# Attention by two head pairs a step, four late token blocks placed by products, and one written order behind the last scores

## The chip, the cores and the metric

The kernel runs on one core of one Trainium2 chip. The metric is the time of one execution on the device, in microseconds (us). The core has TensorE (PE, matrix products and transposes into PSUM), VectorE (DVE), ScalarE (ACT), GpSimd (POOL) and SyncE (SP, which issues most DMAs here). Each engine works through its own instructions in order. PEld is the weight load of TensorE.

## What is computed

Three layers follow one another. Attention is sparse (a query sees 8 global keys and the last 96), its output is the input of a mixture of 8 experts with the two best of each token, and a dense layer with a mish-like activation ends it.

```
scores = scale * q @ k.T + bias          # keep: 8 global keys, 96 local ones
a = softmax(scores);  x = a @ v          # 2 x 768 tokens, 8 heads of 64 -> x is 1536 x 512
noisy = x @ w_gate + log1p(exp(x @ w_noise)) * noise
top2 = two largest of noisy;  top2_w = softmax of them
out[tokens of e] += top2_w * (relu(x @ w1[e]) @ w2[e])       # 8 experts, 512 -> 1024 -> 512
h = out @ w_in;  g = h * tanh(softplus(h));  result = g @ w_out   # 512 -> 2048 -> 512
```

## The kernel before

The 1536 tokens are 12 blocks `t` of 128. Attention takes a block in four steps, one for each pair of heads `hp`; the main loop (lines 734 to 745) calls `st_scores(t, hp)` and then `pipe.run()`. `Steps` (the name `pipe`) is a list of calls by due step: `st_scores` puts `st_exp` into the same step and `st_turn` two steps on, `st_turn` puts `st_av` one step on, `st_av` puts `st_x` one step on. So four steps lie between the scores of a head pair and its last transpose.

- `st_scores` makes two score products into two PSUM banks (`sp`), and VectorE turns each into logits with its smallest value (line 491; here called a reduce). `st_exp` is two exponentials on ScalarE (line 503).
- `st_turn` is four transposes (`tp`, line 516) and a ScalarE copy (`at`, 517). `st_av` is four products with the values (`xp`, 530) and a VectorE copy (`xt`, 534). `st_x` transposes back (`xr`, 541); behind the last head pair of a block come `xs` (548, the finished block), its store, the gate products (564) and, a step later, `st_logits` (576).
- Routing (`st_logits`, `st_route`, `st_rank`) is some 16 to 20 small VectorE operations for a group of blocks (`GROUPS`). They wait in `Fill` and are let out one or three at a time (`PACE`) behind reduces and copies. `st_rank` gives each token of the block its place in the list of an expert, and `lay` (689) is the 0/1 matrix of places of expert 0.
- The rows of expert 0 are gathered for blocks 0 to 8 (`st_first_list`, four indirect DMAs of GpSimd) and turned by products with the identity (`st_first_in`, 654). Blocks 9 to 11 (`LATE` = 9) are added by products of `xs`, split into a high and a low part (`xsh` on ScalarE, `xsl` on GpSimd, 559), with `lay` (`st_first_add`, 664). The result goes to `xgT` (669, 670), with which the first expert product (`first_layer`, 767 to 769) starts.
- Behind the last scores (t = 11, hp = 3) nothing new comes into the pipeline. `pipe.drain` runs what is due, step after step, and lets out what is left in `Fill`.
- Weights are loaded as 128x1024 pieces and split into a high part (`whi`, ScalarE, 264) and a low part (`wlo`, 267). Three of these splits come in blocks 5 to 7, with the low part on GpSimd; the later ones have it on VectorE.

Of the kernel before, what the change touches and what calls it, by code (L numbers as in the profile page):

```python
# [9 lines left out]
F32 = mybir.dt.float32  # L10
# [25 lines left out]
GROUPS = ((0,1,2,3),(4,5,6,7,8),(9,10),(11,))  # L36
MOST = max(len(g) for g in GROUPS)
LATE = 9
# [3 lines left out]
FIRST = (2, 4)  # L42
ORDER = ((0, (0,)), (2, (0,)), (0, (1,)), (2, (1,)), (0, (2, 3)), (2, (2, 3)))
# [65 lines left out]
class Steps:  # L109


    def __init__(self):
        self.at, self.now = {}, 0

    def put(self, ahead, fn, *a, rank=9):
        self.at.setdefault(self.now + ahead, []).append((rank, fn, a))

# [15 lines left out]
class Fill:  # L133
# [3 lines left out]
    def __init__(self):  # L137
        self.ops, self.later, self.hold = deque(), deque(), False
# [7 lines left out]
    def some(self, n, more=0):  # L146

        if not self.ops:
# [15 lines left out]
def build(tc, ctx, I, out, n_global, n_local, dbg=None):  # L164
# [189 lines left out]
    with ExitStack() as st:  # L354
        at1 = st.enter_context(tc.tile_pool(name="at1", bufs=1))
        ld = st.enter_context(tc.tile_pool(name="ld", bufs=2))
        ps_s = st.enter_context(tc.tile_pool(name="ps_s", bufs=PSS if NKP == 512 else 1, space=PSUM))
# [102 lines left out]
        rtc = ps_x.tile([P, 512], F32, name="rtc") if PSS == 2 else rtb  # L460
# [5 lines left out]
        xsp, lay, lgs, es = {}, {}, {}, {}  # L466
# [4 lines left out]
        def st_scores(t, hp):  # L471
# [3 lines left out]
            z = wk.tile([P, 2, NKM], F32, name="z", bufs=4 if early else 3)  # L475
            sm = wk.tile([P, 2], F32, name="sm", bufs=4)
            if hp == 0:
                sums[t] = wk.tile([P, H], F32, name="sums", bufs=3)
            sps = {}

            def product(h):
                sps[h] = ps_s.tile([P, NKP], F32, name="sp")
                hh = slice(h * D, (h + 1) * D)
                for c, kc, n in runs[i]:
                    T.matmul(sps[h][:, c:c + n], raw[t][hh, hp, :], ks[hh, hp, kc:kc + n],  # L485
                             start=(c % 512 == 0), stop=(c + n == nk or (c + n) % 512 == 0))

            for h in range(2):
                for k in ((0, 1) if h == 0 else ()) if NKP == 512 else (h,):
                    product(k)  # L490
                V.tensor_tensor_reduce(out=z[:, h, :nk], in0=sps[h][:, :nk], in1=table(i, 2 * hp + h), scale=-SCALE,
                                       scalar=3e38, op0=OP.add, op1=OP.min, accum_out=sm[:, h:h + 1])
                fill.some(PACE[t >= LATE], MORE[t >= LATE])
            if early and t == NT - 1 and hp == HP - 1:
                lay["chunks"] = [(*CHUNKS[c], d) for d0, cs in ORDER for c in cs for d in (d0, d0 + 1)]
                pipe.put(2, st_first_in, FIRST[0])
            pipe.put(0, st_exp, t, hp, z, sm)
            pipe.put(2, st_turn, t, hp, z, rank=0)

        def st_exp(t, hp, z, sm):  # L500
            nk = NK[t % NB]
            for h in range(2):
                A.activation(z[:, h, :nk], z[:, h, :nk], AF.Exp, bias=sm[:, h:h + 1], scale=-1.0,
                             accum_out=sums[t][:, 2 * hp + h:2 * hp + h + 1])

        def st_turn(t, hp, z):
            nk = NK[t % NB]
            nch = (nk + P - 1) // P
            at = wk.tile([P, (NKM + P - 1) // P, 2, P], F32, name="at")
            for c0 in range(0, nch, 2):  # L510
                cs = range(c0, min(nch, c0 + 2))
                tp = ps_t.tile([P, 2, 2, P], F32, name="tp")
                for c in cs:
                    col = 0 if c == 0 else nk - P * (nch - c)
                    for h in range(2):
                        T.transpose(tp[:, c - c0, h, :], z[:, h, col:col + P], ident)  # L516
                A.activation(at[:, c0:c0 + len(cs)], tp[:, :len(cs)], AF.Copy)
            pipe.put(1, st_av, t, hp, at, rank=2)
            if early and t == NT - 1 and hp == HP - 1:
                pipe.put(1, st_first_in, FIRST[1])  # L520

        def st_av(t, hp, at):
# [3 lines left out]
            xp = xpb[:, hp]  # L526
            for c in range(nch):
                kk = nk - P * (nch - 1) if c == 0 else P
                for h in range(2):
                    T.matmul(xp[h * D:(h + 1) * D, :], vt[:kk, c, (2 * hp + h) * D:(2 * hp + h + 1) * D],  # L530
                             at[:kk, c, h, :], start=(c == 0), stop=(c == nch - 1))
            if hp == 0:
                xts[t] = wk.tile([P, HP, P], F32, name="xt", bufs=2)
            V.tensor_copy(xts[t][:, hp, :], xp)
            fill.some(PACE[t >= LATE], MORE[t >= LATE])
            pipe.put(1, st_x, t, hp, rank=1)

        def st_x(t, hp):
            if hp == 0:
                xps[t] = ps_r.tile([P, HP, P], F32, name="xr")  # L540
            T.transpose(xps[t][:, hp, :], xts[t][:, hp, :], ident)
            if hp == 1:
# [3 lines left out]
            if hp == HP - 1:  # L546
# [4 lines left out]
                pipe.put(2 if t + 1 < NT else 0, nc.sync.dma_start, xd[1 + t * P:1 + (t + 1) * P, :], xs.rearrange("p h d -> p (h d)"))  # L551
                pipe.put(0, st_gate, t)
                if early and t >= LATE:
# [755 lines left out]
```

## Time and profile before

| | |
|---|---|
| median of 3 runs | 764.21 us (762.32 to 766.95) |
| profiled execution | 765.73 us, of which the span 763.9 us |
| attention, from the first scores to the last | 7.35 to 102.8 us of the span |
| behind the last scores, to the end of the first expert product | 102.8 to 126.7 us |
| experts, then dense layer | the rest |
| busy in the span | PE 724.5, PEld 636.3, DVE 601.4, ACT 384.9, POOL 162.8 us |

How to read it: the span is from the first to the last instruction of the profiled execution, and 1.8 us lie around it. TensorE is busy 95% of the span, so what can be saved is where it waits, where its clock is low, or where it does work that can be left out.

### The profile page before, as it was taken

The numbers are of one execution on the slowest core, as the hardware profiler recorded it, in microseconds if no ns is written. First come the engines' busy times: TensorE is split into PE (matmuls) and PEld (weight loads), VectorE is DVE, ScalarE is ACT, GpSimd is POOL, SyncE is SP. The second block draws the span as 40 slices with busy tenths as digits, with TensorE's granted clock in tenths as the row PEclk, the third lists the DMA queues.
The fourth block names the chain that finished last, engine by engine and source line by source line (L and its number), as shares of the span: only waits on it lengthen the run. The fifth ranks groups of instructions, "written<-read, shape, count | busy, mean of one in ns | idle before, by whom it ended". The sixth has DMA issues, their size and how long they took to land.

```text
span 763.9 us, 11872 instructions
## 1 busy us (share of the span) xinstructions
PE 724.5 (95%) x4257; PEld 636.3 (83%) x4257; DVE 601.4 (79%) x1297; ACT 384.9 (50%) x814; POOL 162.8 (21%) x167
## 2 busy tenths in 40 slices
PE   8999989999999999999999999888899999999995
PEld 4665669899998989899999987766789898989894
DVE  7677767986768575757676597999999999999985
ACT  5787742344444444444444446444555555555453
POOL 2012030210101020101100031555333424432221
PEclk9999989999999999999999999999999999999999
DMA  6677421556655564646554552311020111101001
GB/s 173 201 190 183 141 76 44 169 194 195 189 168 190 166 193 152 210 155 214 165 183 139 179 196 79 105 55 28 1 69 29 29 42 27 32 26 42 1 0 46
DMA packets 42935, 89.28 MB, mean 117 GB/s; under 512 B 5987, under 2 KB 18403, under 8 KB 42868
## 3 DMA queue, kind: packets, MB, share of 16 engines
q1 hardware_dynamic: 35412, 69.37, 29.4%
q0 software_dynamic: 4096, 13.11, 5.8%
q10 hardware_dynamic: 3360, 5.97, 2.1%
q8 instruction: 35, 0.57, 0.3%
q14 instruction: 32, 0.26, 0.1%
HBM read 75.32 MB, written 13.11 MB: 116 GB/s over the span
## 4 chain that ended last, share of the span: by engine, by line
PE 64%; DVE 18%; ACT 6%; DMA 6%; issue 4%; POOL 1%; ACTq 1%; POOLq 0%; DVEq 0%
PE hp L767 8%; PE hp L768 8%; PE hp L769 8%; DMA raw<-in_w_moe 5%; PE ac L1133 4%; PE ac L1134 4%; PE ac L1138 4%; PE sp L485 4%; PE ac L767 4%; PE ac L769 4%; PE ac L768 4%; PE xp L530 3%; PE tp L516 3%; DVE wlo L267 3%; DVE yT L1090 2%
## 5 line engine op out<-in xcount | busy, mean ns | idle before, releaser
L1106 POOL TENSOR_TENSOR yT<-yT 128x384 f32<-128x384 f32 (+1 forms) x68 | 71.5, 1051 | 191.0 <-DVE yT L1105 173.3
L767 PE MATMUL hp<-xgh,whi 128*128 128x416 f32 (+1 forms) x288 | 104.3, 362 | 0.0
L267 DVE TENSOR_TENSOR wlo<-raw,whi 128x1024 fp32r<-128x1024 f32 x61 | 74.6, 1223 | 34.8 <-ACT whi L264 34.1
L769 PE MATMUL hp<-xgh,wlo 128*128 128x416 f32 (+1 forms) x288 | 100.8, 350 | 0.0
L768 PE MATMUL hp<-xgl,whi 128*128 128x416 f32 (+1 forms) x288 | 100.7, 350 | 0.0
L767 PE MATMUL ac<-hhi,whi 128*128 128x416 f32 x256 | 91.7, 358 | 0.0
L768 PE MATMUL ac<-hlo,whi 128*128 128x416 f32 x256 | 90.0, 352 | 1.5 <-DVE hlo L814 1.5
L769 PE MATMUL ac<-hhi,wlo 128*128 128x416 f32 x256 | 89.8, 351 | 0.0
L1109 ACT ACTIVATE hhi<-yT 128x384 fp32r<-128x384 f32 (+1 forms) x68 | 34.4, 506 | 93.8 <-POOL yT L1106 93.8
L314 POOL DMA_INDIRECT xg<-xd,gidx x32 | 32.2, 1005 | 219.7 <-PE tq L801 196.9
L767 PE MATMUL hp<-xgh,whil 128*128 128x384 f32 x224 | 76.4, 341 | 0.0
L768 PE MATMUL hp<-xgl,whil 128*128 128x384 f32 x224 | 75.7, 338 | 0.5 <-DVE xgl L773 0.5
L769 PE MATMUL hp<-xgh,wlol 128*128 128x384 f32 x224 | 75.3, 336 | 0.0
L264 ACT ACTIVATE whi<-raw 128x1024 fp32r<-128x1024 f32 x64 | 67.5, 1054 | 8.5 <-ACT ys L849 6.9
L1090 DVE SCALAR_TENSOR_TENSOR yT<-yT 128x384 f32<-128x384 f32 (+1 forms) x68 | 63.2, 929 | 2.3
L1133 PE MATMUL ac<-whil,hhi 128*128 128x512 f32 x144 | 58.2, 404 | 2.1 <-ACT hhi L1109 2.0
L813 ACT ACTIVATE hhi<-hp 128x416 fp32r<-128x416 f32 x64 | 32.6, 510 | 49.0 <-PE hp L769 46.7
L1134 PE MATMUL ac<-wlol,hhi 128*128 128x512 f32 x144 | 56.6, 393 | 0.0
L768 PEld LDWEIGHTS hp<-xgl,whi 128*128 128x128 f32 x288 | 54.3, 189 | 0.9 <-DVE xgl L670 0.3
L767 PEld LDWEIGHTS hp<-xgh,whi 128*128 128x128 f32 x288 | 54.1, 188 | 0.8
L769 PEld LDWEIGHTS hp<-xgh,wlo 128*128 128x128 f32 x288 | 54.0, 188 | 0.5
L295 ACT ACTIVATE whil<-t 128x512 fp32r<-128x512 f32 x26 | 16.4, 633 | 73.5 <-DVE t L301 65.9
(241 smaller groups left out, 1625.4 us busy)
## 6 DMA issues: line engine op xcount, KB each, us to landing
raw<-in_w_moe SPq DMA_DIRECT2D x96, 512.0 KB
yd<-ys ACTq DMA_DIRECT2D x21, 256.0 KB
ks<-in_k_t SPq DMA_DIRECT2D x24, 136.0 KB
qr<-in_q_t SPq DMA_DIRECT2D x24, 128.0 KB
vt<-in_v_w SPq DMA_DIRECT2D x12, 256.0 KB
xd<-xs SPq DMA_DIRECT2D x12, 256.0 KB
out<-ys SPq DMA_DIRECT2D x12, 256.0 KB
vt<-in_v_w SPq DMA_DIRECT2D x10, 208.0 KB
```

What stands on the lines that cost most here:

```text
L264: A.activation(hi, raw, AF.Copy)
L267: e_lo.tensor_tensor(lo, raw, hi.bitcast(F32), op=OP.subtract)
L314: G.indirect_dma_start(out=xg[:n], out_offset=None, in_=xd[:1 + blocks * P], in_offset=bass.IndirectOffsetOnAxis(ap=idx, axis=0))
L767: T.matmul(ps, whi, xhi, start=first, stop=False)
L768: T.matmul(ps, whi, xlo, start=False, stop=False)
L769: T.matmul(ps, wlo, xhi, start=False, stop=last)
L813: A.activation(hhi, hp[:, :CAP], AF.Relu)
L1090: V.scalar_tensor_tensor(t, v, 2.0, v, op0=OP.add, op1=OP.mult)
L1106: G.tensor_tensor(v, v, t, op=OP.mult)
L1109: A.activation(g[0][:, cc], m[1][:, cc], AF.Copy)
L1133: T.matmul(acc2[tb][c], ghi[:, cc], whi, start=(f == 0), stop=False)
L1134: T.matmul(acc2[tb][c], ghi[:, cc], wlo, start=False, stop=False)
```

## The change

1. A step takes two head pairs (`PER` = 2). The four score products of a step share the same two PSUM banks, 256 columns each; `st_turn` is due one step on and not two; the copy `xt` takes both pairs at once. Three double steps (six pairs) lie between the scores and the last transpose.
2. The low parts of the three early weight splits go from GpSimd to VectorE, and so does `xsl`.
3. `LATE` is 8. Blocks 8 to 11 are put in by products, and blocks 0 to 7 by the gather. The groups of routing are (0..3), (4..7), (8, 9), (10, 11).
4. Behind the last scores, `drain()` takes every step by name in a written order.

```diff
-GROUPS = ((0,1,2,3),(4,5,6,7,8),(9,10),(11,))
+GROUPS = ((0, 1, 2, 3), (4, 5, 6, 7), (8, 9), (10, 11))
...
-LATE = 9
+LATE = 8
...
+            for hp in hps if NKP == 512 else ():
+                for h in range(2):
+                    product(hp, h)
+            for hp, (z, sm) in zip(hps, zs):
+                for h in range(2):
...
+                    V.tensor_tensor_reduce(out=z[:, h, :nk], in0=sps[h][:, hp - hp0, :nk], in1=table(i, 2 * hp + h),
+                                           scale=-SCALE, scalar=3e38, op0=OP.add, op1=OP.min, accum_out=sm[:, h:h + 1])
+                    fill.some(PACE[t >= LATE], MORE[t >= LATE])
...
+            pipe.put(0, st_exp, t, hps, zs)
+            pipe.put(1 if early else 2, st_turn, t, hps, zs, rank=0)
...
+            pipe.put(1, st_av, t, hps, ats, rank=3)
...
-            V.tensor_copy(xts[t][:, hp, :], xp)
...
+            V.tensor_copy(xts[t][:, hps[0]:hps[-1] + 1, :], xpb[:, hps[0]:hps[-1] + 1])
...
-            G.tensor_tensor(xsp[t][1], xf, xsp[t][0].bitcast(F32), op=OP.subtract)
...
+        def st_xsl(t):
+            V.tensor_tensor(xsp[t][1], xsf[t], xsp[t][0].bitcast(F32), op=OP.subtract)
...
+        def st_first_add(t):
+
+            for x in xsp[t]:
+                for d in range(4):
+                    T.matmul(lay["banks"][d][:, :CAP], x[:, d * P:(d + 1) * P], lay[t], start=False,
+                             stop=(t == NT - 1 and x is xsp[t][1]))
...
+            r9 = take()
+            go("st_x")
+            go("st_gate")
+            go("st_store")
+            go("st_av")
+            run(r9[:3])
+            go("st_turn")
+            go("st_logits")
+            l10 = take()
+            go("st_x")
+            run(l10 + r9[3:6])
+            st_xsh(NT - 2)
+            go("st_av")
+            st_first_in(2)
+            st_gate(NT - 1)
+            run(r9[6:])
+            st_first_in(2)
+            go("st_logits")
+            r11 = take()
+            run(r11[:3])
+            go("st_x")
+            go("st_store")
+            run(r11[3:6])
+            st_xsh(NT - 1)
+            go("st_rank")
+            k9 = take()
+            st_first_in(99)
+            run(k9[:2])
+            run(r11[6:])
+            st_first_add(LATE)
+            go("st_rank")
+            k11 = take()
+            run(k9[2:3])
+            st_first_add(LATE + 1)
+            run(k11[:2])
+            st_xsl(NT - 2)
+            st_first_add(NT - 2)
+            run(k11[2:3])
+            st_xsl(NT - 1)
+            st_first_add(NT - 1)
+            st_first_out()
+            run(k9[3:] + k11[3:])
+            fill.rest()
+            run(slots_of(LATE, NT - LATE))
...
-            for hp in range(HP):
+            for hp in range(0, HP, PER):
...
-                    w_split(A, G)
+                    w_split(A, V)
...
-        pipe.drain(fill)
+        if not early:
+            pipe.drain(fill)
+        else:
+            drain()
```

In the rows of order below, `x4` is four instructions of one kind; `sp` are score products, `tp` transposes of the exponentials, `xp` products with the values, `xr` transposes back, `rt` gate products and logits, `oh` the marks of the two best experts.

TensorE in the middle of attention, one step of before:

```order
L485 MATMUL sp<-ks_125,qr 128x232 x2
L516 MATMUL tp<-ident,z 128x128 x4
L541 MATMUL xr<-ident,xt 128x128
L530 MATMUL xp<-at,vt 64x128 x4
L564 MATMUL rt<-xt,wgn 32x128 x4
```

and one step of the changed kernel at the same place:

```order
L504 MATMUL sp<-ks_125,qr 128x232 x4
L544 MATMUL tp<-ident,z 128x128 x8
L570 MATMUL xr<-ident,xt 128x128 x2
L557 MATMUL xp<-at,vt 64x128 x8
L603 MATMUL rt<-xt,wgn 32x128 x4
```

A step holds twice the products in the same succession, and each transpose of exponentials stands one step behind its scores and no longer two.

VectorE from block 6 to block 7, where the second weight split comes; before (`ge` and `r` are routing):

```order
L548 TENSOR_TENSOR xs<-xr,sums 128x512
L534 COPY xt<-xp 128x128
L491 ISA z,sm<-sp,tab_0_184 128x232
L491 ISA sm 128x1
L622 TENSOR_TENSOR ge<-noisy,best 128x4
```

and in the changed kernel:

```order
L561 COPY xt<-xp 128x256
L648 SCALAR_TENSOR_TENSOR r<-r 128x32
L649 TENSOR_TENSOR r<-r 128x32
L282 TENSOR_TENSOR wlo<-raw,whi 128x1024
L514 ISA z,sm<-sp,tab_0_184 128x232
L514 ISA sm 128x1
```

The low part of the weights now stands on VectorE, ahead of the reduces of the next step; before it was in the queue of GpSimd and VectorE had reduces, copies and routing alone.

TensorE behind the last scores; before:

```order
L485 MATMUL sp<-ks_126,qr 128x232 x2
L516 MATMUL tp<-ident,z 128x128 x4
L541 MATMUL xr<-ident,xt 128x128
L530 MATMUL xp<-at,vt 64x128 x4
L564 MATMUL rt<-xt,wgn 32x128 x4
L516 MATMUL tp<-ident,z 128x128 x4
L541 MATMUL xr<-ident,xt 128x128
L530 MATMUL xp<-at,vt 64x128 x4
L576 MATMUL rt<-ident,gt 128x128
L516 MATMUL tp<-ident,z 128x128 x4
L541 MATMUL xr<-ident,xt 128x128
L530 MATMUL xp<-at,vt 64x128 x4
```

and in the changed kernel:

```order
L504 MATMUL sp<-ks_126,qr 128x232 x4
L544 MATMUL tp<-ident,z 128x128 x8
L570 MATMUL xr<-ident,xt 128x128 x2
L611 MATMUL rt<-ident,gt 128x128
L557 MATMUL xp<-at,vt 64x128 x8
L570 MATMUL xr<-ident,xt 128x128 x2
L603 MATMUL rt<-xt,wgn 32x128 x4
L557 MATMUL xp<-at,vt 64x128 x8
L544 MATMUL tp<-ident,z 128x128 x8
L611 MATMUL rt<-ident,gt 128x128
L570 MATMUL xr<-ident,xt 128x128 x2
L557 MATMUL xp<-at,vt 64x128 x8
```

More is left behind the last scores now: four head pairs to turn instead of three, eight back transposes instead of five, six pairs of value products instead of four, three logits instead of two. The list and the gather stand ahead of the last scores in both.

## Rows read from the trace of the kernel before

**Rows 1.** Busy time by stretch: PE, PEld, DVE, ACT, POOL, then granted clock, DMA share, GB/s.
```profile
75.00:100.00 25.00, 25.00 (x237) 16.42 (x231) 18.03 (x91) 19.19 (x66) 1.28 (x1) 1.00 0.40 122
...
63.70:67.60 3.90, 3.90 (x21) 2.13 (x17) 2.76 (x15) 2.77 (x11) 0.00 (x0) 0.56 0.83 200
...
109.10:113.00 3.90, 3.87 (x22) 2.67 (x22) 3.56 (x20) 0.81 (x3) 0.93 (x2) 0.50 0.07 28
```
**Rows 2.** Timeline of TensorE, an undisturbed step: start, duration, line, tiles, [idle before <-releaser].
```profile
75.16 0.66 PE L485 MATMUL sp<-ks,qr 64*128 64x232 f32 x4
75.75 0.66 PE L516 MATMUL tp<-ident,z 128*128 128x128 f32 x4
76.25 0.27 PE L541 MATMUL xr<-ident,xt 128*128 128x128 f32 x1
76.45 0.66 PE L530 MATMUL xp<-at,vt 104*64 104x128 f32 x8
77.04 0.43 PE L564 MATMUL rt<-xt,wgn 128*32 128x128 f32 x8
77.39 0.66 PE L485 MATMUL sp<-ks,qr 64*128 64x232 f32 x4
```
**Rows 3.** Timeline of all engines around two of the early weight splits.
```profile
51.37 2.36 POOL L267 TENSOR_TENSOR wlo<-raw,whi 128x1024 fp32r<-128x1024 f32 x1 [46.14 <-ACT whi L264]
...
51.58 2.19 DVE L610 TENSOR_SCALAR r<-r 128x32 f32<-128x32 f32 x1
...
54.02 0.80 PE L485 MATMUL sp<-ks,qr 64*128 64x128 f32 x4 [0.42 <-DVE sm L491]
...
62.06 0.33 PE L576 MATMUL rt<-ident,gt 128*128 128x128 f32 x1 [1.18 <-DVE lh L583]
```
**Rows 4.** Timelines of ScalarE and VectorE: copy, exponential, both halves of a weight split.
```profile
91.50 0.58 ACT L517 ACTIVATE at<-tp 128x512 f32<-128x512 f32 x1
91.98 0.48 ACT L503 ACTIVATE z<-z,sm 128x232 f32<-128x232 f32 x1
...
129.61 1.05 ACT L264 ACTIVATE whi<-raw 128x1024 fp32r<-128x1024 f32 x1
...
134.65 1.22 DVE L267 TENSOR_TENSOR wlo<-raw,whi 128x1024 fp32r<-128x1024 f32 x1
```
**Rows 5.** Chain that ended last, in order of time: start, duration, what.
```profile
81.48 0.90 PE sp L485 x4
```
**Rows 6.** Timeline of TensorE from block 11 to the first expert product.
```profile
98.49 1.05 PE L485 MATMUL sp<-ks,qr 64*128 64x232 f32 x4
...
102.17 0.66 PE L485 MATMUL sp<-ks,qr 64*128 64x232 f32 x4
...
116.94 1.17 PE L654 MATMUL sp<-ident,xg 128*128 128x128 f32 x8
...
124.27 0.34 PE L767 MATMUL hp<-xgh,whi 128*128 128x416 f32 x1
...
126.53 0.35 PE L769 MATMUL hp<-xgh,wlo 128*128 128x416 f32 x1
```
**Rows 7.** Timeline of VectorE behind the last scores.
```profile
108.78 0.29 DVE L534 COPY xt<-xp 128x128 f32<-128x128 f32 x1 [3.17 <-PE tp L516]
...
111.16 0.17 DVE L610 TENSOR_SCALAR r<-r 128x16 f32<-128x16 f32 x1
...
112.94 0.15 DVE L622 TENSOR_TENSOR ge<-noisy,best 128x2 f32<-128x2 f32 x1
...
115.34 0.69 DVE L548 TENSOR_TENSOR xs<-xr,sums 128x512 f32<-128x512 f32 x1 [1.37 <-PE xr L541]
...
127.88 0.59 DVE L814 SCALAR_TENSOR_TENSOR hlo<-hp,hhi 128x416 fp32r<-128x416 f32 x1 [0.58 <-ACT hhi L813]
```
**Rows 8.** Timeline of ScalarE behind the last scores.
```profile
106.51 0.28 ACT L567 ACTIVATE gt<-rt 128x128 f32<-128x128 f32 x1 [1.46 <-PE xp L530]
...
127.33 0.52 ACT L813 ACTIVATE hhi<-hp 128x416 fp32r<-128x416 f32 x1 [2.25 <-DVE slots L639]
```

More of the change, by code (lines that the diff above doesn't have):

```diff
@@ L474, in st_scores @@
             ks = kst[t // NB]
[L475 to L478, printed above, removed]
+            hps = range(hp0, hp0 + PER)
+            zs = [(wk.tile([P, 2, NKM], F32, name="z", bufs=4 if early else 3), wk.tile([P, 2], F32, name="sm", bufs=4))
+                  for _ in hps]
+            if hp0 == 0:
+                sums[t] = wk.tile([P, H], F32, name="sums", bufs=4)
@@ new lines, in st_scores, with st_exp @@
+            end = hp0 + PER == HP
+            if early and t == NT - 1 and end:
+                lay["chunks"] = [(*CHUNKS[c], d) for d0, cs in ORDER for c in cs for d in (d0, d0 + 1)]
+                fill.some(99)
+                fill.off = True
+            pipe.put(0, st_exp, t, hps, zs)
+            pipe.put(1 if early else 2, st_turn, t, hps, zs, rank=0)
+        def st_exp(t, hps, zs):
+            nk = NK[t % NB]
+            for hp, (z, sm) in zip(hps, zs):
+                for h in range(2):
+                    A.activation(z[:, h, :nk], z[:, h, :nk], AF.Exp, bias=sm[:, h:h + 1], scale=-1.0,
+                                 accum_out=sums[t][:, 2 * hp + h:2 * hp + h + 1])
@@ L507, in st_turn @@
+        def st_turn(t, hps, zs):
             nk = NK[t % NB]
             nch = (nk + P - 1) // P
[L509 to L522, printed above, removed]
+            ats = [wk.tile([P, (NKM + P - 1) // P, 2, P], F32, name="at", bufs=2 * PER) for _ in hps]
+            for at, (z, _) in zip(ats, zs):
+                for c0 in range(0, nch, 2):
+                    cs = range(c0, min(nch, c0 + 2))
+                    tp = ps_t.tile([P, 2, 2, P], F32, name="tp")
+                    for c in cs:
+                        col = 0 if c == 0 else nk - P * (nch - c)
+                        for h in range(2):
+                            T.transpose(tp[:, c - c0, h, :], z[:, h, col:col + P], ident)
+                    A.activation(at[:, c0:c0 + len(cs)], tp[:, :len(cs)], AF.Copy)
@@ L673, in st_rank, with st_first_out @@
+        def st_first_out():
+            xgT[0] = parts()
+            for d in range(4):
+                A.activation(xgT[0][0][:, d], lay["banks"][d][:, :CAP], AF.Copy)
+                V.tensor_tensor(xgT[0][1][:, d], lay["banks"][d][:, :CAP], xgT[0][0][:, d].bitcast(F32),
+                                op=OP.subtract)
         def st_rank(t, n, ge):
-            rp = (xpb[:, 0] if t == NT - 1 else rtc[:, 128:])[:, :n * E].rearrange("p (t e) -> p t e", e=E)
+            rp = (xpb[:, 0] if t + n == NT else rtc[:, 128:])[:, :n * E].rearrange("p (t e) -> p t e", e=E)
```

164 lines of the change are left out of this document (79 added, 85 removed).

## The prediction

> **What bounds the kernel now.** I read the busy time by stretch first, then the timeline of TensorE, then what it waits for. In the middle of attention TensorE is busy the whole time at a granted clock of 1.00, VectorE 18.0 of 25 us, ScalarE 19.2 [rows 1]. One step of one head pair is 0.59 us of scores, 0.50 of transposes until the back transpose starts, 0.20 for that, 0.59 of value products and, once in a block, 0.35 of gate, each the distance between two starts [rows 2]. So a step is 1.88 us, and a block with gate and logits (some 0.26) 8.13. Two head pairs a step are the same work for an engine that is already full: **the doubling by itself saves nothing.** What can be saved are the places at which TensorE is not full: blocks 6 and 7, single late reduces, and the stretch from the last scores (end 102.17 + 0.59 = 102.76) to the end of the first expert product (126.53 + 0.19 = 126.72), 23.96 us [rows 6]. Behind that stretch the program is unchanged, and I let it shift as a whole.
>
> **1. The low parts leave GpSimd: -3.3 us.** A GpSimd subtraction runs from 51.37 to 53.73. A VectorE operation on 32 columns that starts at 51.58 ends at 53.77, 2.19 us, where the same line takes 0.17 elsewhere [rows 3, 7]. The next reduces wait behind it, and TensorE waits 0.42 at 54.02, and at the next split 1.18 at 62.06 [rows 3]. [...] The other reading is that routing simply fills VectorE there, and then nothing of this goes away; I take the first since one tiny operation lasts until the GpSimd one ends. [...]
>
> **2. The same low parts on VectorE: +1.3 us.** Each is 1.22 us [rows 4], in front of the next reduces, and it waits for the high part, which ScalarE makes behind two copies and four exponentials. Count from the start of a step's scores: the second head pair's transposes end 4 x 0.59 = 2.37 later, the copies (0.48 each) at 2.95, four exponentials of 0.47 at 4.83, the high part (1.0) at 5.85, the low part (1.15) at 7.05. Without it the reduces of the next step would start at 5.0, so they are 2 us late. Scores need their two banks back, that is the third and fourth reduce, about 1.5 to 2 us after the first. The step after next is due at 8.1 for a full block; for block 6, whose steps have only 128 keys and are shorter, earlier. I get no wait for the first split, 0.8 us for the second and 0.5 for the third. Bounds: 0 if routing leaves the slots empty, 3 if each costs 1 us.
>
> **3. Late reduces in blocks 9 to 11: -0.8 us.** Scores that take 0.90 instead of 0.59 at 81.48 [rows 5] and 1.05 at 98.49 [rows 6] wait for a bank behind routing; there is another of the first size. With four reduces per two pairs the banks have some 1 us of slack per step. Bounds -1.2 and 0. At the start of the program, with nothing else to do between, the longer steps cost me +0.2 (0 to 0.6).
>
> **4. The doubled step in the middle: 0.** The transpose now stands one step behind its scores. From above, exponentials of a step are done at 4.83, and the next step's second transposes are due at 4.06 + 1.19 + 0.59 = 5.84; the first pair's at 5.25 against 3.9. About 1 us of slack hides it; if that cover were gone, each 0.1 us would cost 22 steps x 0.1 = 2.2 us.
>
> **5. Behind the last scores: -2.7 us.** The order leaves more behind: one pair of transposes, three back transposes, two value products and one logits more than before, 0.59 + 0.6 + 1.18 + 0.26 = 2.6 us. So the last scores come 2.6 us earlier, and the question is how long the rest is. From the end of the last scores, in the written order, with the steps of [rows 2]:
> - TensorE turns (1.18), back transposes (0.4), logits, values (1.18): 3.0. VectorE copies two pairs; 256 columns are not in the trace; 128 take 0.29, and 512 in another operation 0.69 [rows 7], so 0.29 to 0.69, I take 0.42. Then back transposes, gate, values of block 11's first half: 5.7; turns of its second half: 6.9, logits and back transposes 7.5. The copies on ScalarE stand behind the exponential of routing, and the last values end at 8.8, their copy at 9.25. (The first reduce waits for the third score product, since both pairs share a bank; I count 0.25 us for that.)
> - Then routing of (8, 9) on VectorE: from 111.16 to 113.09, 1.93 us for the same ten operations [rows 7]; marks at 11.1. Block 11's logits, `xs` (0.69) and the first mask follow, 2.2 us, then the ten operations again: marks of (10, 11) at 15.3.
> - From 11.1 TensorE is full: ranks 0.4, twelve identity products (four take at most 1.17 [rows 6]) 3.0, and 32 products of late blocks, at the pitch of the first expert product, (126.53 - 124.27) / 12 = 0.19, that is 6.1, with the second ranks 0.4 between. End 21.0. The masks and low parts on VectorE (0.3 to 0.7 each) are in time.
> - High parts, low parts and the first expert product: the order now closes all four banks together, so the product ends 2.85 later: 23.9.
>
> 23.9 against 23.96, with 2.6 us more in it: -2.7. The eight extra products of block 8 (1.5 us) are inside. Two waits of before for which I see no cause in the order, 1.46 us of ScalarE and 3.17 of VectorE [rows 7, 8], I have not carried over, nor the clock of 0.50 behind them [rows 1]. Bounds: -3.2 if identity products and masks all hide; +1.8 if such waits (1.5 to 2.5) or such a clock (4 us at half, 2 lost) come again.
>
> **6. Slots before the first hidden copy: +0.9.** The first `hhi` waits for the last slot operation [rows 8], which now stands behind more of them: twelve small ones instead of seven, at the 0.2 a piece of routing [rows 7] 2.4 us instead of 1.4; `hlo` follows 0.55 later [rows 7, 8]. Before, `hlo` was done at 128.47 and its reader, behind a second product of 2.26, due at 128.98 [rows 6, 7]; now the reader waits 0.6, and the lists that VectorE makes next lose 0.3 more. Bounds 0 and 1.5.
>
> **Sum.** -3.3 + 1.3 - 0.8 + 0.2 - 2.7 + 0.9 = -4.4. Against the profiled execution's own 765.73 (span 763.9 and 1.8 around it) that is 761.3; this execution is 1.5 above the median of 764.21, and the forecast for the median is **759.8 us**.
>
> **Rivals.**
> - **The stretch behind the last scores stumbles again:** waits like those of [rows 7, 8] or a clock at its lower level in the full part of TensorE. For it: the gather with its GpSimd work is still there, and nothing in the order explains those waits. Against: TensorE has fewer holes in the new order. +2.2: 762.0.
> - **The GpSimd was not the cause** in blocks 6 and 7, so the change doesn't do there what it seems to: routing remains, 3.3 are not saved: 763.1. Against it speaks 0.17 against 2.19.
> - **The transposes wait for exponentials (slower).** In a double step the chain transposes, copy, four exponentials, transposes must stay under 4.06 us. I count 3.0 to 3.1, and ScalarE at 77% [rows 1] leaves little more. If the second pair's exponentials came 1.4 us later than I count, each of 22 steps would lose 0.4 us, 8.8 in all: 768.6. It decides from 1 us on.
> - **Better:** no wait from the splits on VectorE and all bounds of 5 on the good side: 757.5.
>
> [...]
>
> **How the numbers follow.** Forecast 0.47, stumble 0.22, GpSimd not the cause 0.11, transposes wait 0.10, better 0.10. Some 0.5% (3.8 us, here 760.4 and 768.0) is about what a measurement of this kernel can tell from no change. The forecast lies 0.6 us on the faster side, with bounds of some 3 us to both sides: I give it 0.6 faster, 0.4 same. With better, and a tenth of the others: faster 0.28 + 0.10 + 0.05 + 0.01 = 0.44; same 0.19 + 0.17 + 0.10 + 0.03 = 0.49; slower 0.07. The predicted time is the likeliest case's; the range 756 to 765.5 leaves out most of the slower case and the far ends of the others.
>
> **What would show it.** Blocks 6 and 7: no VectorE operation of 2 us, TensorE's waits under 0.8 us, clock 1.00. Middle blocks: 8.13 us each. Last scores ending some 97.6 us into the span, and 24 us from there to the end of the first expert product. Wrong would be: `tp` waiting for `z` in every step, or the 0.50 clock in the stretch of the late products.

## The result, and the profile of the changed kernel

| | before | changed |
|---|---|---|
| median of 20 runs each, taken together | 769.26 us (762.32 to 777.42) | 760.28 us (756.57 to 765.03) |
| ratio, 95% interval | | 0.9898 (0.9874 to 0.9922) |
| span of the profiled execution | 763.9 us | 758.5 us |
| start of the last scores | 102.17 us [rows 6] | 90.55 us |
| end of the first expert product (12 products) | 126.72 us [rows 6] | 118.94 us |

The change makes the kernel 1.0% faster, some 7.8 us (6.0 to 9.7); the forecast said 0.6%. The ratio and its interval compare the fast runs alone, while the medians above hold all runs and lie 9.0 us apart. That 759.8 us was so close to 760.28 is partly luck: the forecast started from a median of three runs, 764.21 us, and twenty runs put the kernel before at 769.26.

**Middle blocks.** Timeline of TensorE in the changed kernel (start, duration, line, tiles):

```profile
24.35 1.05 PE L504 MATMUL sp<-ks,qr 64*128 64x232 f32 x8
25.34 1.09 PE L544 MATMUL tp<-ident,z 128*128 128x128 f32 x8
26.27 0.38 PE L570 MATMUL xr<-ident,xt 128*128 128x128 f32 x2
26.58 1.10 PE L557 MATMUL xp<-at,vt 104*64 104x128 f32 x16
27.61 0.43 PE L603 MATMUL rt<-xt,wgn 128*32 128x128 f32 x8
```

From start to start a double step is 0.99 + 0.93 + 0.31 + 1.03 = 3.26 us. Two single steps took 2 x 1.88 = 3.76 [rows 2]. The products are the same, and TensorE shows as busy all the time in both. A block takes 6.98 us (27.96 to 34.94) instead of 8.13. The forecast had no gain here at all.

**Blocks 5 to 7.** There is no VectorE operation of 2 us any more, as forecast, but TensorE waits at each of the three splits:

```profile
49.50 0.92 PE L504 MATMUL sp<-ks,qr 64*128 64x128 f32 x8 [0.69 <-DVE sm L514]
...
57.27 1.43 PE L504 MATMUL sp<-ks,qr 64*128 64x232 f32 x8 [1.25 <-DVE sm L514]
...
65.56 1.37 PE L504 MATMUL sp<-ks,qr 64*128 64x232 f32 x8 [0.62 <-DVE sm L514]
```

Together 2.56 us, where 1.3 were forecast.

**Behind the last scores.** Busy time by stretch (PE, PEld, DVE, ACT, POOL, granted clock, DMA share, GB/s), then TensorE and VectorE around the first expert product:

```profile
99.00:112.40 13.40, 13.10 (x113) 11.69 (x113) 8.41 (x39) 2.55 (x8) 0.21 (x1) 1.00 0.17 61
112.40:115.00 2.60, 0.23 (x2) 0.00 (x0) 2.36 (x7) 1.44 (x4) 0.00 (x0) 1.00 0.00 0
115.00:119.00 4.00, 3.96 (x13) 3.83 (x14) 1.77 (x14) 0.00 (x0) 0.24 (x1) 0.57 0.00 0
```

```profile
112.08 0.55 PE L695 MATMUL tp<-lay,xsl 128*128 128x416 f32 x2
115.04 0.43 PE L854 MATMUL hp<-xgh,whi 128*128 128x416 f32 x1 [2.41 <-DVE base L726]
...
118.72 0.39 PE L856 MATMUL hp<-xgh,wlo 128*128 128x416 f32 x1
```

```profile
114.73 0.17 DVE L726 SCALAR_TENSOR_TENSOR base<-xp,base 128x16 f32<-128x16 f32 x1
```

The clock is 1.00 in the stretch of the late products, where the kernel before had 0.50 [rows 1] behind its wait of 3.17 us [rows 7]; that wait is not in this execution, and it comes up again below. Then TensorE stands still for 2.41 us, until a 0.17 us operation of VectorE (`base`) has read the bank that `hp` takes over, and the products behind that stand 0.35 us apart and not 0.19 [rows 6], at a clock of 0.57.

**Further on.** At the first expert product the changed kernel is 7.8 us ahead, at the end 5.4. Up to some 428 us the lead stays between 7.3 and 8.1; then, in code that the change leaves alone, the expert stage loses 1.9 us between 434 and 460 us. Timeline of TensorE there, before and changed:

```profile
455.49 1.83 PE L933 MATMUL hp<-ident,xgl 128*128 128x128 f32 x14 [0.85 <-DVE xgl L926]
```
```profile
449.67 3.19 PE L1020 MATMUL hp<-ident,xgl 128*128 128x128 f32 x14 [0.86 <-DVE xgl L1013]
```

These fourteen products run at a granted clock of 0.53 (449.67 to 452.9 us), where the kernel before has 1.00 (455.49 to 457.4). Whether that comes from the change is not shown. I take the difference at the first expert product, 7.8 us, for what the change does; the 7.8 us that the ratio gives agree with it.

### The profile page after: what moved, and what is told of

Read it like the earlier page. It is cut to its first block, busy times and chain, and to the rows that moved or that the text cites. A ratio compares the mean times of both kernels' runs of the same rounds, so it can differ in the third digit from the quotient of the medians.

```text
span 758.5 us, 11859 instructions
## 1 busy us (share of the span) xinstructions
PE 713.6 (94%) x4259; PEld 640.2 (84%) x4259; DVE 599.6 (79%) x1280; ACT 382.9 (50%) x815; POOL 152.3 (20%) x161
## 4 chain that ended last, share of the span: by engine, by line
PE 60%; DVE 19%; ACT 9%; DMA 6%; issue 4%; ACTq 1%; POOL 1%; POOLq 0%; DVEq 0%
PE hp L854 8%; PE hp L855 8%; PE hp L856 8%; DMA raw<-in_w_moe 5%; PE ac L1220 4%; PE ac L1221 4%; PE ac L1225 4%; PE ac L855 4%; PE ac L854 4%; PE ac L856 4%; DVE wlo L282 3%; DVE yT L1177 3%; ACT whi L279 2%; DVE t L316 2%; PE sp L504 2%
## 5 line engine op out<-in xcount | busy, mean ns | idle before, releaser
L282 DVE TENSOR_TENSOR wlo<-raw,whi 128x1024 fp32r<-128x1024 f32 x64 | 78.3, 1224 | 37.8 <-ACT whi L279 37.1
```

What stands on the lines that cost most here:

```text
L282: e_lo.tensor_tensor(lo, raw, hi.bitcast(F32), op=OP.subtract)
```

## Experiments

### Does a change of the kind of product cost TensorE time?

The rival is that the middle blocks gained through fewer and longer operations on the other engines. Both runs keep every product and every operation of the other engines, and only interleave transposes and value products (blocks 0 to 10) by pair, and by half pair (the edit below is that of the first).

```diff
-            pipe.put(1 if early else 2, st_turn, t, hps, zs, rank=0)
+                pipe.put(1, st_turn, t, hps[:1], zs[:1], ats, rank=0)
+                pipe.put(1, st_turn, t, hps[1:], zs[1:], ats, rank=2)
...
-                pipe.put(1, st_av, t, hps, ats, rank=3)
+                    pipe.put(1, st_av, t, pair, both, 0, rank=1.5)
+                    pipe.put(1, st_av, t, pair, both, 1, rank=3)
```

> The changed kernel in blocks 0 to 10 with TensorE's products of a double step in the order scores of both pairs, transposes of pair 0, xr, values of pair 0, transposes of pair 1, values of pair 1: the same products, with 6 changes from one kind of product to another in a double step instead of 4 (the kernel before has 8 in two steps). The copies of xt on VectorE stay one for both pairs. Theory A (each change of kind costs TensorE time: 3.76 us for 8 changes before, 3.25 us for 4 after, so 0.13 us each): a double step of the middle blocks takes 3.50 us, a block 7.5 instead of 6.98, ten blocks 5 us more; ratio to before about 0.997. Theory B (the saving came from fewer and longer operations on the other engines, which this leaves as they are): a double step stays at 3.25 us, ratio 0.990. Theory C (the transposes or values now wait for ScalarE's copies, which are 88 percent busy there): waits of TensorE on ACT appear in the middle blocks, and the step is longer by those waits.

> As kinds_by_pair, but the transposes and values are also taken in turn by halves of a pair (the two key chunks): 10 changes of kind in a double step instead of 4, the same products. Theory A (0.13 us for each change): a double step takes 3.25 + 6 x 0.13 = 4.0 us, a block 8.5, ten blocks 15 us more than the changed kernel; ratio to before about 1.009. If the price of a change depends on the two kinds, between 0.07 and 0.2 us each, 3.7 to 4.45 us a double step. Theory B (the other engines): 3.25 us, ratio 0.990. Theory C: waits on ACT for the copies of the transposes, seen as such in the rows.

Timeline of TensorE, by pair, one double step:

```profile
27.68 1.05 PE L504 MATMUL sp<-ks,qr 64*128 64x232 f32 x8
28.66 0.66 PE L549 MATMUL tp<-ident,z 128*128 128x128 f32 x4
29.15 0.38 PE L586 MATMUL xr<-ident,xt 128*128 128x128 f32 x2
29.47 0.66 PE L571 MATMUL xp<-at,vt 104*64 104x128 f32 x8
30.06 0.66 PE L549 MATMUL tp<-ident,z 128*128 128x128 f32 x4
30.64 0.66 PE L571 MATMUL xp<-at,vt 104*64 104x128 f32 x8
```

| kernel | changes of kind in a block | us a block | ratio to before (95%) |
|---|---|---|---|
| changed | 8 | 6.98 | 0.9898 (0.9874 to 0.9922) |
| by pair | 12 | 7.58 (24.01 to 31.59) | 0.9974 (0.9945 to 1.0003) |
| before | 16 | 8.13 | 1 |
| by half pair | 20 | 9.06 (26.40 to 35.46) | 1.0104 (1.0071 to 1.0136) |

(Gate and logits stand once in each block of all four and are not counted.) In both runs TensorE shows no wait between 20 and 48 us. One is hidden by half pair, in one of the two double steps of a block, where the weights of the second transpose wait for an exponential:

```profile
27.78 0.14 PEld L554 LDWEIGHTS tp<-ident,z 128*128 128x128 f32 x1 [0.26 <-ACT z L540]
```

These two transposes take 0.66 us to the next product (27.38 to 28.04), where others take 0.37, so 0.29 of the 9.06 us is theory C. Theory A holds for the rest, with 0.14 to 0.15 us for each change: (7.58 - 6.98) / 4 = 0.15, (8.13 - 6.98) / 8 = 0.14, (9.06 - 0.29 - 6.98) / 12 = 0.15. Half of the saving of the middle blocks is gone with the first run, and with it most of what the change gained.

Where the time sits is seen on the engine that loads weights. PEld before, then in the changed kernel:

```profile
75.16 0.30 PEld L485 LDWEIGHTS sp<-ks,qr 64*128 64x128 f32 x4 [0.17 <-issue]
75.75 0.42 PEld L516 LDWEIGHTS tp<-ident,z 128*128 128x128 f32 x4 [0.29 <-ACT z L503]
76.14 0.14 PEld L541 LDWEIGHTS xr<-ident,xt 128*128 128x128 f32 x1
76.45 0.42 PEld L530 LDWEIGHTS xp<-at,vt 104*64 104x64 f32 x8 [0.17 <-issue]
```
```profile
24.35 0.69 PEld L504 LDWEIGHTS sp<-ks,qr 64*128 64x128 f32 x8 [0.17 <-issue]
25.34 0.86 PEld L544 LDWEIGHTS tp<-ident,z 128*128 128x128 f32 x8 [0.29 <-ACT z L530]
26.16 0.25 PEld L570 LDWEIGHTS xr<-ident,xt 128*128 128x128 f32 x2
26.58 0.86 PEld L557 LDWEIGHTS xp<-at,vt 104*64 104x64 f32 x16 [0.17 <-issue]
```

At every change of the tile shape (the 64\*128 ahead of the sizes) in these rows the weight load idles 0.17 to 0.29 us and then starts together with the first product, so nothing is loaded ahead. From `tp` to `xr`, both 128\*128, it doesn't idle. The number of such holes is halved and their size is the same. Counted by tile shape, with gate and logits, the blocks of the table have 7, 11, 14 and 19 changes, and each costs 0.15 to 0.16 us. Why the load idles there, these rows do not show; the forecast did not weigh such a price.

### What did the low parts cost, and what do they cost on VectorE?

Three kernels: the one before with only the low parts moved to VectorE (terms 1 and 2 alone); the same with each low part written two steps later; and the changed kernel with the low parts back on GpSimd.

```diff
-                    w_split(A, G)
+                    w_split(A, V)
```

> The kernel before with only the low parts of the three weight splits moved from GpSimd to VectorE. As forecast (terms 1 and 2 at the old pace): 3.3 us go, 0.0, 0.8 and 0.5 us of new waits come for the three splits: net 2.0 us less, ratio to before 0.9974. By the waits that the changed kernel showed at its faster pace (0.69, 1.25, 0.62): net 0.7 us less, ratio 0.999. If the size of those waits comes from the faster pace of TensorE in the changed kernel, they are near the forecast here; if it comes from the length of the low part alone (1.23 us behind 1.05 us of ScalarE), they are 2.6 us here too. Rival (GpSimd never was the cause): VectorE's 2.2 us operation and TensorE's half clock about 54 us stay, ratio 1.000 to 1.003.

Ratio 1.0073 (1.0033 to 1.0112): slower, the opposite of the forecast for these two terms. In the kernel with this one edit, VectorE, TensorE and the busy time by stretches of 2 us (between 54 and 56 us the clock is at 0.66 on average):

```profile
51.31 1.22 DVE L267 TENSOR_TENSOR wlo<-raw,whi 128x1024 fp32r<-128x1024 f32 x1 [1.48 <-ACT whi L264]
```
```profile
52.91 0.91 PE L485 MATMUL sp<-ks,qr 64*128 64x128 f32 x4 [1.27 <-DVE sm L491]
```
```profile
56.00:58.00 2.00, 2.00 (x11) 1.44 (x13) 1.00 (x8) 0.31 (x1) 0.00 (x0) 0.50 1.06 193
...
...
74.00:76.00 2.00, 1.74 (x13) 1.16 (x12) 1.42 (x2) 1.15 (x2) 0.00 (x0) 0.72 0.92 288
```

VectorE idles 1.48 us in front of a low part whose high part is not ready, TensorE then waits 1.27 us where the forecast had "no wait for the first split", and behind it the granted clock is at its lower level (0.50) for 20 us. The last scores start at 109.64 us, 7.5 later than before. The low part does cost something on VectorE, then, and the larger price is the low clock behind that wait. That the wait alone brings it on is not shown: behind waits of 1.25 us in the changed kernel, 1.28 with its low parts on GpSimd and 1.39 in a version below, the clock stayed at 1.00.

```diff
+                if early and hp == 0 and t in (6, 7, 8):
+                    low()
...
-                    w_split(A, G)
+                    low = w_split(A, V, later=True)
```

> The kernel before with the low parts of the three early weight splits on VectorE, each written two steps (of one head pair) after its high part, behind that step's reduces, instead of on GpSimd right behind the high part. Theory A (GpSimd's operations cost 3.3 us in blocks 6 and 7 as forecast in term 1; moving the low parts to VectorE right behind the high part was worse, ratio 1.0073, only because each one waited at the head of VectorE's queue for ScalarE, and one such wait of 1.27 us was followed by 20 us at the lower clock): no VectorE operation of 2 us, no wait of TensorE on sm above 0.4 us in blocks 5 to 7, clock 1.00 from 48 to 91 us, 2.5 to 3.5 us less than the kernel before, ratio 0.9955 to 0.9970. Theory B (the old pace of single steps leaves VectorE no room for 3 x 1.23 us, wherever they stand): waits of 0.5 us and more and a low clock appear again one or two steps later, ratio 1.003 or more.

Ratio 0.9969 (0.9932 to 1.0005), some 2.4 us less by an interval that reaches past 1, and the last scores start at 100.20 us instead of 102.17. A stretch of that run, the one with its longest hole:

```profile
62.00:66.00 4.00, 3.84 (x26) 2.44 (x22) 3.97 (x23) 3.17 (x11) 0.00 (x0) 1.00 0.86 244
```

From block 5 to the last scores there is no hole of more than 0.16 us, and the clock stays at 1.00. By the trace theory A holds, below the lower end of its size: taking the low parts off GpSimd is worth some 2 us, which the time alone does not tell from nothing, provided that they don't stand at the head of VectorE's queue waiting for ScalarE.

```diff
-                    w_split(A, V)
+                    w_split(A, G)
```

> The changed kernel with the low parts of the three weight splits in blocks 5 to 7 back on GpSimd; all else as changed. As forecast (terms 1 and 2): GpSimd's 2.2 to 2.4 us operation is back, VectorE operations beside it take up to 2 us, TensorE loses 3.3 us in two or three places with part of that at the lower clock, and the 1.3 us of waits behind the low parts on VectorE go: net 2.0 us more than the changed kernel. As the trace of the changed kernel has it: the waits of 0.69, 1.25 and 0.62 us (2.6 us) go, and 3.3 us come: net 0.7 us more. Rival (GpSimd never was the cause): the changed kernel's 2.6 us of waits go, nothing comes, 2 to 3 us less than the changed kernel, ratio to before about 0.986.

Ratio 0.9884 (0.9833 to 0.9934), not to be told from the changed kernel's 0.9898. By the trace the last scores start at 88.66 us, 1.9 *earlier* than in the changed kernel, where two of the three numbers expected have them later and the rival's alone earlier, by 2 to 3; the 1.9 are lost again behind them, through a wait that is treated below. GpSimd does hold VectorE up, but once and not three times. GpSimd, then VectorE, beside the first two splits (behind the first, TensorE waits 1.28 us at 50.73):

```profile
47.63 2.36 POOL L282 TENSOR_TENSOR wlo<-raw,whi 128x1024 fp32r<-128x1024 f32 x1 [42.40 <-ACT whi L279]
...
55.19 2.37 POOL L282 TENSOR_TENSOR wlo<-raw,whi 128x1024 fp32r<-128x1024 f32 x1 [5.20 <-ACT whi L279]
```
```profile
47.70 2.33 DVE L641 TENSOR_SCALAR r<-e 128x32 f32<-128x32 f32 x1 [0.43 <-ACT e L627]
...
55.83 0.16 DVE L651 MAX8 best<-noisy 128x8 f32<-128x8 f32 x1
55.91 0.38 DVE L514 CUSTOM_DVE_ANT_0 z<-sp,tab 128x232 f32<-128x232 f32 x1
```

The operation on 32 columns lasts as long as GpSimd's (2.33 and 2.36 us); beside the second of GpSimd's operations, a maximum (0.16) and a reduce (0.38) take their usual time. What sets the operations that are held apart from those that are not is not shown. The kernel before has a second held operation, beside the GpSimd subtraction that ends at 61.47 us and ahead of the wait of 1.18 [rows 3]; with the low parts on GpSimd in the changed kernel the same operation, with no subtraction beside it, takes 0.16:

```profile
60.28 1.20 DVE L622 TENSOR_TENSOR ge<-noisy,best 128x4 f32<-128x4 f32 x1
```

So in these traces what a GpSimd operation costs depends on which VectorE operation falls beside it, and what the forecast charged to GpSimd came from what the old order happened to put there.

### Is it the bank that `base` reads, and is the low clock only a consequence?

```diff
             st_first_add(NT - 1)
+            run(k9[3:] + k11[3:])
             st_first_out()
-            run(k9[3:] + k11[3:])
```

> The changed kernel with the two base updates of the last groups written ahead of the copies of the collected rows (xgh, xgl) instead of behind them. Theory A: the first expert product waits 2.41 us only because the bank it takes over is still to be read by base at 114.73 us, and the lower clock (0.57 from 115 to 119 us) is a consequence of that wait. Then the first product starts about 112.6 us, right behind the first xgh, the wait on base is gone, the clock stays at 1.00, products stand 0.19 us apart or wait for an xgl (the last ends about 114.8), and the 12 products of the first expert step end at about 115.3 instead of 118.9: 3.0 to 3.7 us less than the changed kernel, ratio to before about 0.985. Theory B: the collected rows bound the stage, since the fourth xgl ends at 114.7 whatever base does, and the clock falls in any case because the engine idles: 12 products end at about 117.5, 1 to 1.5 us less, ratio about 0.988. Theory C: idle there is covered by later work of the expert stage: the first product starts earlier and the span stays at 758.5.

```diff
             st_first_out()
+            busy = ps_r.tile([P, 512], F32, name="xr")
+            for _ in range(9):
+                T.matmul(busy, ones, dense, start=True, stop=True)
             run(k9[3:] + k11[3:])
```

> The changed kernel with nine products of constants (the warm-up form, 128x512 bf16, 0.37 us each at the start of the program at its clock there) put on TensorE into the 2.41 us wait for base; the wait itself stays. They write a bank that nothing reads. Theory A (the lower clock comes from the idle): the first expert product starts as before at about 115.0 us or up to 0.3 later, but the clock stays 1.00, the 12 products stand 0.19 us apart instead of 0.35, and end at about 117.4 instead of 118.9: about 1.5 us less than the changed kernel. Theory B (the clock falls for another reason, at that point of the program): rows 0.35 apart again, and the span is the same or some tenths longer.

TensorE with `base` early, then with the wait filled by products:

```profile
115.78 0.54 PE L695 MATMUL tp<-lay,xsl 128*128 128x416 f32 x2
116.36 0.46 PE L854 MATMUL hp<-xgh,whi 128*128 128x416 f32 x1
116.99 0.46 PE L855 MATMUL hp<-xgl,whi 128*128 128x416 f32 x1 [0.17 <-DVE xgl L702]
...
119.00 0.35 PE L856 MATMUL hp<-xgh,wlo 128*128 128x416 f32 x1
```
```profile
115.08 2.12 PE L811 MATMUL xr<-dense,ones 128*128 128x512 bf16 x9
117.66 0.43 PE L857 MATMUL hp<-xgh,whi 128*128 128x416 f32 x1 [0.45 <-DVE base L726]
...
120.02 0.35 PE L857 MATMUL hp<-xgh,whi 128*128 128x416 f32 x1
```

From the end of the last late product to the end of the twelve products of the first expert step it takes 6.5 us in the changed kernel (112.46 to 118.94), 3.0 with `base` early (116.16 to 119.19) and 4.9 with the wait filled (115.08 to 120.02). So in these traces the wait for the bank costs 2 us and the low clock behind it 1.5, as theory A of both runs has it: with products in the wait the following ones stand 0.19 us apart, though the wait is as long. That the products did this is not shown by one trace, since the kernel by half pair has the same wait, unfilled, and no low clock behind it (twelve products in 2.36 us, where the changed kernel takes 3.90):

```profile
133.94 0.43 PE L889 MATMUL hp<-xgh,whi 128*128 128x416 f32 x1 [2.41 <-DVE base L761]
...
136.30 0.35 PE L889 MATMUL hp<-xgh,whi 128*128 128x416 f32 x1
```

Of the five traces with this wait unfilled, four have 3.4 us at the lower level behind it and one has none; of the four with `base` early or the wait filled, none has it. So the bank as the cause of the wait is shown, and the wait as the cause of the low clock is likely. The ratios are 0.9871 (0.9819 to 0.9923) and 0.9844 (0.9799 to 0.9888): both below the changed kernel's, neither clearly.

The profiled executions hide the gain, since the stretch ahead lost 3.7 and 2.6 us (its end at 116.16 and 115.08 instead of 112.46). With `base` early, TensorE and VectorE:

```profile
97.63 0.66 PE L570 MATMUL xr<-ident,xt 128*128 128x128 f32 x2 [3.66 <-DVE xt L561]
```
```profile
97.15 0.42 DVE L561 COPY xt<-xp 128x256 f32<-128x256 f32 x1 [2.23 <-remote]
```

In the changed kernel's trace the same copy starts at 94.84 without idling, and TensorE waits 1.29. This is the wait of 3.17 us of the kernel before [rows 7], which the forecast left out since nothing in the order explains it. In the eight traces with the new order behind the last scores and the gathers at that place, it is there three times (TensorE waits 3.66, 2.87, 3.64) and not there five times (1.29 in three, 0.99, 0.76). The copy waits by its order for value products that ended over 2 us earlier, and GpSimd's four gather operations run at the same time. Where the wait is there, the copy starts only behind the end of the last gather (97.15 against 96.27 us with `base` early), and 3.4 to 6.8 us at the lower level of the clock come behind it, as in the kernel before; where it is not, the copy starts ahead of the fourth gather and the clock stays at 1.00. I did not find its cause; that the changed kernel's trace is without it may be luck.

### Was the fourth late block worth it?

```diff
-GROUPS = ((0, 1, 2, 3), (4, 5, 6, 7), (8, 9), (10, 11))
+GROUPS = ((0, 1, 2, 3), (4, 5, 6, 7, 8), (9,), (10, 11))
-LATE = 8
+LATE = 9
...
+            r8, r9 = r9[17:], r9[:17]
+            run(r8)
...
+            go("st_first_list")
```

> The changed kernel with blocks 9 to 11 put to their places by products, as before the change, instead of 8 to 11: block 8 is gathered with the others, in groups of 4, 5, 1 and 2 blocks, the list and the gathers stand behind the last scores in the written order. Theory A (the fourth late block pays because the gathers, 4 of 0.95 to 1.2 us on GpSimd and some 3.5 us to landing, start a block earlier): the gathers start at about 95 to 97 instead of 91.4 us, the products that turn their rows wait for them, and in spite of 8 products (8 x 0.19 = 1.5 us) and one mark less the first expert product comes 1 to 4 us later; ratio to before 0.991 to 0.995. Theory B (the gathered rows have time enough either way): the first expert product comes 1.5 to 2 us earlier, ratio about 0.988.

Ratio 0.9884 (0.9812 to 0.9956), no difference that can be told. TensorE in that run:

```profile
100.49 1.22 PE L688 MATMUL sp<-ident,xg 128*128 128x128 f32 x4 [0.36 <-DMA xg<-xd,gidx]
```

The gathers start at 96.84 us instead of 91.41, but their rows are waited for by 0.36 us only. The last scores come 1.9 us earlier (88.65), since routing, list and gather of block 8 now stand behind them, and the first expert product comes 0.2 later (115.24 against 115.04). Neither theory fits: part of the gain went to a clock of 0.50 from 98 to 105 us. That the number of late blocks matters is not shown.

### A version with the two waits taken out

> The changed kernel with two edits: the base updates of the last groups ahead of the copies of the collected rows (as in base_early), and each low part of the three weight splits written on VectorE one double step after its high part, behind that step's reduces, instead of right behind it. Theory A (the waits of 0.69, 1.25 and 0.62 us come from a low part that waits for ScalarE's high part at the head of VectorE's queue with the next reduces behind it): those three waits go or fall under 0.3 us, the last scores start at about 88.0 instead of 90.55 us, and with the wait on base gone as well the program is 5 to 6 us shorter than the changed kernel, ratio to before about 0.982. Theory B (VectorE is simply full in blocks 5 to 7, 1.2 us more of work is 1.2 us late wherever it stands): waits of the same sum move to the next step; the last scores start at about 90.5, ratio about 0.986, as base_early.

> As base_early_low_later (ratio 0.9783), but each low part is made in two halves of 512 columns, one in each of the two double steps behind the high part. There one whole low part of 1.22 us at 56.75 us let TensorE wait 1.39 us for the logits at 59.26, and another 0.31 at 67.68. Theory A (the length of the single operation in front of routing decides): the first wait falls to 0.8 us or less, the last scores start 0.5 to 0.8 us earlier than 88.89, ratio 0.977 to 0.978. Theory B (routing and the reduces of that step fill VectorE without the low part): the wait stays at 1.2 to 1.4 us, ratio 0.978 to 0.980.

The first: `base` early, and each low part of the splits one double step behind its high part. The second: that low part in two halves, in two double steps.

```diff
+                if early and hp == 0 and t in (6, 7, 8):
+                    low(slice(0, 512))
+                if early and hp == 2 and t in (6, 7, 8):
+                    low(slice(512, 1024))
...
-                    w_split(A, V)
+                    low = w_split(A, V, later=True)
```

TensorE in the first, then in the second:

```profile
59.26 0.33 PE L614 MATMUL rt<-ident,gt 128*128 128x128 f32 x1 [1.39 <-DVE lh L621]
...
88.89 1.05 PE L507 MATMUL sp<-ks,qr 64*128 64x232 f32 x8
```
```profile
58.14 0.33 PE L616 MATMUL rt<-ident,gt 128*128 128x128 f32 x1 [0.85 <-DVE lh L623]
...
87.78 1.05 PE L509 MATMUL sp<-ks,qr 64*128 64x232 f32 x8
```

The ratios are 0.9783 (0.9726 to 0.9841) and 0.9822 (0.9797 to 0.9848), medians 754.4 and 754.81 us; the two can't be told apart by time. Both lie wholly below the changed kernel's 0.9898 (0.9874 to 0.9922), so both beat it and the kernel before. The waits of 0.69, 1.25 and 0.62 us at the scores are gone in the first, with one of 1.39 and one of 0.31 in their place; the halves bring 1.39 down to 0.85, a little above the 0.8 expected. So a part of the waits only moved, as theory B has it: 2.56 us in sum became 1.70 and 1.16. The last scores start 1.7 and 2.8 us earlier than in the changed kernel, the twelve products end at 113.86 and 112.72 us instead of 118.94. Neither trace has the wait of the copy, or the lower clock level between the last scores and the first expert product.

## The forecast, step by step

The direction and the size were about right, by terms that were wrong in both directions. Up to the last scores the forecast had 5.2 us (2.6 of them moved behind these scores); the trace has 11.2 (their end at 91.54 instead of 102.76). From there to the end of the first expert product it had no change; the trace has 3.4 us more (27.4 instead of 23.96).

- **What bounds the kernel, and term 4 (0): wrong, and the largest miss.** "Two head pairs a step are the same work for an engine that is already full" takes a busy TensorE for one at its peak. What failed is the step from "busy" to "nothing to save": fewer changes of kind give 1.15 us in each full middle block, in sum more than the 6.0 us by which the forecast missed up to the last scores (longer waits in blocks 5 to 9 took part of it back). That is 0.14 to 0.15 us for each change of kind, shown by undoing it in two doses. The forecast read 0.50 us for four transposes as their price; eight cost 0.93, four score products 0.59 and eight 0.99, eight value products 0.59 and sixteen 1.03. So some 0.07, 0.19 and 0.15 us in a group are paid once. Rows of PEld would have shown it beforehand.
- **Term 1 (-3.3): right in kind, somewhat large.** No run shows its 3.3 us: 1.60 of them are waits that can be read (0.42 and 1.18 [rows 3]), and the other 1.7 are an estimate of what the granted clock of 0.56 over 3.9 us [rows 1] cost. Alone, and without the wait that term 2 brings, it measures some 2 us in the kernel before (2.0 by the trace; 2.4 by the time, which does not exclude 0). In the changed order GpSimd would cost less: one operation of VectorE is blocked, and the last scores come 1.9 us earlier with the low parts on GpSimd.
- **Term 2 (+1.3): too small.** 2.56 us in the changed kernel (0.69, 1.25 and 0.62 for forecast 0, 0.8 and 0.5), within the bound of 3. The step that failed is "no wait for the first split": the low part idles at the head of the queue (1.16 us of VectorE in front of the first one) while the reduces of the next step are behind it, and the shorter steps want these earlier. In the kernel before the same low parts cost much more, by the clock; the sum of terms 1 and 2, -2.0, is refuted there with some +5.6 us (ratio 1.0073; why the clock fell there is open).
- **Term 3 (-0.8, startup +0.2): plausible, not tested.** No scores wait behind 66 us in the changed kernel. One double step waits for its exponentials instead, 0.87 us at 78.55: the rival "transposes wait" in one place and not in 22 steps.
- **Term 5 (-2.7): the walk held, up to its last line.** From the end of the last scores (91.54), forecast and trace: last value products end +8.8 and +8.5, first marks +11.1 and +10.8, second marks +15.3 and +14.5, late products end +21.0 and +20.9. The line that failed is "high parts, low parts and the first expert product": 27.4 instead of 23.9. Its 2.85 us stand there without a working and measured 6.5. The forecast asked when the operands are ready and not who still reads the bank of `hp`. The first reduce, counted 0.25 us late for the third score product, starts 1.19 us behind the start of the last scores (90.55 to 91.74); in a single step of before it was 0.69 (75.16 to 75.85), so 0.50 later. (The pitch of 0.19 divides 11 distances by 12 and came out right by luck: [rows 6] give 0.21 on average, with two long ones at the start, and the late products stand 0.19 apart.)
- **Term 6 (+0.9): the wrong wait.** The slots do stand later, ending at 116.94, but the first `hhi` at 119.19 waits for TensorE. The wait that the forecast looked for on ScalarE came 4 us earlier, on TensorE, through `base`, and was 2 us with 1.5 of low clock.
- **Rivals.** "Stumbles again" took place, by a wait that it did not name, and its price of 2.2 us was exceeded (3.5); the old unexplained wait is there in three of eight traces with the new order. It was hidden by what term 4 gave. The 757.5 of "better" is not the sum of its parts: 1.3 and 0.5 off 759.8 give 758.0.

## What to carry to other kernels

TensorE at 100% busy still gained 1.15 us a block here from putting products of the same tile shape side by side: read the idle time of the weight load at each change of kind, and count the changes. Before an operation is written behind the last step of a stage, look at which bank it still reads and who takes that bank next (here TensorE, which waited 2.41 us). A low part that waited 1.48 us for ScalarE at the head of VectorE's queue held the reduces behind it, and TensorE waited 1.27; written later, the same low parts left no wait above 0.16 us in the kernel before, and 1.70 instead of 2.56 us in the changed one.

## What the runs showed of the hardware

- A change of tile shape between products cost 0.15 to 0.16 us on average in these fp32 products (blocks with 7, 11, 14 and 19 changes), with PEld idle 0.17 to 0.29 us at each in the rows shown and not between two kinds of the same shape.
- In blocks 5 to 7, one wait of TensorE of 1.27 us was followed by 20 us at the lower clock level (0.50), with TensorE busy throughout (the kernel before with the low parts on VectorE), and waits of 1.18 us (the kernel before) and 1.61 us (by half pair) by 3.4 and 6.8 us of it; behind waits of 1.25, 1.28 and 1.39 us in three other traces the clock stayed at 1.00. Why it fell in some and not in others is open.
- A wait of 2.3 to 2.4 us ahead of the first expert product was followed by 3.4 us at the lower level in four traces (0.35 us a product) and by none in a fifth (0.19). With nine products without use in the wait, one trace has 0.19.
- Beside a GpSimd subtraction of 2.36 us, VectorE operations on 32 columns lasted 2.19 us (the kernel before) and 2.33 us (the changed one with the low parts on GpSimd), and one on 4 columns 1.20 us (the kernel before), each until the subtraction ended; a maximum (0.16) and a reduce that reads PSUM (0.38) took their usual time (the changed one with the low parts on GpSimd).
